# Retention and two feed-forward layers on one core: the first loads on two queues, and TensorE in the program's order during the first tile

## The chip, the cores and the metric

One core of a Trainium2 chip runs the whole program. The metric is the device time of one execution in microseconds (us); each number given as a time of a kernel is a median of several executions, and the trace is that of one further execution. The engines are TensorE (PE in the rows, with PEld for its weight loads), VectorE (DVE), ScalarE (ACT), GpSimd (POOL) and SyncE (SP), which here only issues transfers.

## The reference

Retention over 4 batches, 8 heads, 576 positions and 64 dimensions a head feeds a first feed-forward layer (a gate h*cos(h)) and then a second one (a normalisation, a gate silu(g)*val). Cut to what matters:

```python
scores = scale * np.matmul(q, k.transpose(0, 1, 3, 2))
gamma = 1.0 - 2.0 ** (-5.0 - np.arange(H, dtype=np.float32))
Dmat = np.where(rel >= 0, gamma[:, None, None] ** rel[None, :, :], 0.0)
x = np.matmul(scores * Dmat[None], v)              # -> 2304 tokens x 512
h = x @ w_in                                       # 512 -> 2048
x = (h * np.cos(h)) @ w_out                        # 2048 -> 512
xn = x / np.sqrt(np.mean(x * x, -1, keepdims=True) + 1e-06) * rms_g
g, val = xn @ w_gate, xn @ w_val                   # 512 -> 1536
out = (g * (1.0 / (1.0 + np.exp(-g))) * val) @ w_out2
```

## The kernel before

**Retention.** The 576 positions of a batch are cut into five chunks (four of 128 positions and one of 64), so there are 20 chunks, numbered n. A chunk has one load of 1 MB (`x`: k and q turned, v, and k by tokens), issued on SyncE's queue by `load(n)`. Each chunk is worked in four groups of matrix products, and this text names them by letters:

- S(n), in `scores`: the products of k and q, 8 matmuls into two PSUM banks (L249). VectorE multiplies both banks with the triangular mask (L252, two passes) and so frees them.
- T(n), in `values`: k times v is added to the running sum `total` of the batch (L265). Before it GpSimd has scaled v (L244). ScalarE copies `total` into `state` afterwards (L275), which the next chunk reads; the next T may not add to `total` before that copy.
- Q(n): state times q (L270), except for the first chunk of a batch.
- V(n): masked scores times v (L280). VectorE then multiplies the result with the decay table `gam` into `xall` (L283) and so frees the bank.

The decay tables of the four later chunk positions are made once from the first one (`gam0`, loaded from `gq`) by 16 ScalarE instructions (L237).

**First feed-forward layer.** It goes over tiles of 512 tokens and over 16 blocks f of the hidden width. In the first tile (tokens 0 to 511, thus chunks 0 to 3) a step i does H(i), the product of x with the block's first weights (12 matmuls of 512 columns, L187 to L189), a gate, and O(i-3), the product of the gated block with its second weights (12 matmuls of 512 columns into `acc`). In the program O(f) is written three steps after H(f) (`LAG`). The gate is a chain: ScalarE L414, VectorE L415, ScalarE L417 (a sine), VectorE L421, ScalarE L423, VectorE L124. x and the weights are split into a high and a low part: for x four casts on ScalarE (L181) and four subtractions on VectorE (L124), and for each block a conversion of the loaded words: ScalarE L132 and L141, VectorE L136, L137, L142 and L143, ScalarE L159 and VectorE L124 on `w`. All 16 blocks are converted during the first tile.

**How the two are interleaved.** Chunks 0 to 4 come first, in the loop `for n in range(PRO)`. Chunks 5 to 19 are spread over steps 0 to 7 of the first tile, up to two in a step; the program writes a step as H(i), S, O(i-3), T Q V, S, T Q V.

**What sets the order.** Up to the end of the first tile a scheduler orders each engine's instructions by its own model; the order of the source is not kept, on any engine. From then on ScalarE, VectorE and GpSimd keep to the program's order (`manual_schedule(engines=ENGINES)`), and later TensorE too. During retention the results of S, V and H share three PSUM banks (`g`, `bufs=3`), in the order in which the program takes them. SyncE's queue is in the order of `PLAN`: chunks 0 to 3, block 0, chunks 4 and 5, block 1, and so on. Ahead of everything, 10 matmuls on constants (`WARM`) keep TensorE busy until the first data come.

## Time and profile before

| | |
|---|---|
| median of 3 executions | 930.67 us (929.98 to 932.38) |
| the profiled execution, its own time | 928.54 us |
| its span, from the first to the last instruction | 926.7 us |
| TensorE busy | 903.1 us, 97% of the span |
| VectorE, ScalarE, GpSimd busy | 619.6, 462.2, 26.9 us |

The profiled execution took 1.84 us more than its span, and 2.13 us less than the median. The profile's table of forty slices (each 23 us) shows TensorE below nine tenths in the first and the last alone, and VectorE at eight or nine tenths in the second to the seventh, that is in the first tile.

### The profile page before, as it was taken

To read this page: it belongs to the slowest core of one execution; us is meant where nothing else is said; L and a number is where in the kernel's file an instruction comes from. 1 tells how busy PE (TensorE), PEld (TensorE's weight loads), DVE (VectorE), ACT (ScalarE), POOL (GpSimd) and SP (SyncE) were. 2 spreads that over 40 slices of the span, in tenths; PEclk is the share of its full clock that TensorE was granted. 3 is DMA by queue.
4 is the path that set the end of the run, shared out by engine and by line. 5 is a ranking of instruction groups with operands and counts; after the bars stand their busy time and mean duration, and the time that the engine had idled before them with its cause. 6 is when DMAs were issued, how large, how long until landed. Compare 5 with 4: busy or idle time off the path is not lost.

```text
span 926.7 us, 12891 instructions
## 1 busy us (share of the span) xinstructions
PE 903.1 (97%) x4996; PEld 791.0 (85%) x4996; DVE 619.6 (67%) x1022; ACT 462.2 (50%) x816; POOL 26.9 (3%) x27
## 2 busy tenths in 40 slices
PE   7999999999999999999999899999999999999998
PEld 6777788888887888988888799999888999999997
DVE  3999989778888887768657666675456446333332
ACT  4656566576556666367545444444432334322222
POOL 2321100000000000000000000000000000000000
PEclk9999999999999999999999999999999999999999
DMA  8946451035424353202035376676744555755531
GB/s 334 410 186 227 155 224 72 21 117 193 164 98 159 137 159 126 69 1 103 1 148 204 124 297 251 252 268 246 259 176 176 207 209 212 265 206 209 204 132 69
DMA packets 34732, 163.72 MB, mean 177 GB/s; under 512 B 4080, under 2 KB 5232, under 8 KB 23792
## 3 DMA queue, kind: packets, MB, share of 16 engines
q1 hardware_dynamic: 34672, 162.91, 48.0%
q8 instruction: 39, 0.64, 0.3%
q14 instruction: 21, 0.17, 0.1%
HBM read 123.57 MB, written 39.32 MB: 176 GB/s over the span
## 4 chain that ended last, share of the span: by engine, by line
PE 79%; DVE 14%; ACT 4%; issue 2%; DMA 1%; SPq 0%; ACTq 0%; DVEq 0%
PE h L743 27%; PE acc L715 15%; PE acc L187 8%; PE acc L188 8%; PE acc L189 8%; PE h L189 3%; PE h L188 3%; PE h L187 3%; DVE r L421 1%; DVE t L142 1%; DVE t L143 1%; PE g L280 1%; DVE r L415 1%; PE g L249 1%; PE g L270 1%
## 5 line engine op out<-in xcount | busy, mean ns | idle before, releaser
L743 PE MATMUL h<-w 128*128 128x384 f32 x1224 | 230.5, 337 | 6.6 <-ACT s L750 2.6
L743 PEld LDWEIGHTS h<-w 128*128 128x128 f32 x1224 | 214.9, 188 | 15.2 <-ACT s L750 5.3
L715 PE MATMUL acc<-w,shi 128*128 128x512 f32 x432 | 134.3, 392 | 0.0
L187 PE MATMUL acc<-ghi,w 128*128 128x512 f32 (+1 forms) x320 | 117.4, 373 | 2.8 <-ACT xall L614 1.7
L188 PE MATMUL acc<-glo,w 128*128 128x512 f32 (+1 forms) x320 | 117.6, 369 | 0.1
L189 PE MATMUL acc<-ghi,w 128*128 128x512 f32 (+1 forms) x320 | 117.3, 368 | 0.0
L750 ACT COPY s<-h 128x384 f32<-128x384 f32 x108 | 51.9, 480 | 128.1 <-PE h L743 128.0
L715 PEld LDWEIGHTS acc<-w,shi 128*128 128x128 f32 x432 | 80.1, 188 | 13.4
L417 ACT ACTIVATE r<-r,half_pi 128x512 f32<-128x512 f32 (+1 forms) x80 | 54.5, 681 | 65.5 <-DVE r L415 65.2
L763 DVE TENSOR_TENSOR sg<-s,h 128x384 f32<-128x384 f32 x54 | 29.9, 553 | 85.6 <-PE h L743 45.4
L715 PE MATMUL acc<-w,slo 128*128 128x512 f32 x216 | 85.4, 395 | 0.0
L775 ACT CAST shi<-v 128x384 fp32r<-128x384 f32 x72 | 37.0, 514 | 70.3 <-DVE v L771 70.3
L124 DVE TENSOR_TENSOR glo<-r,ghi 128x512 fp32r<-128x512 f32 (+1 forms) x78 | 49.6, 636 | 33.4 <-ACT ghi L423 31.6
L187 PEld LDWEIGHTS acc<-ghi,w 128*128 128x128 f32 x320 | 59.4, 188 | 14.5 <-ACT xall L614 2.8
L423 ACT CAST ghi<-r 128x512 fp32r<-128x512 f32 (+1 forms) x80 | 46.2, 577 | 48.2 <-DVE r L421 46.9
L189 PEld LDWEIGHTS acc<-ghi,w 128*128 128x128 f32 x320 | 60.3, 188 | 10.1
L188 PEld LDWEIGHTS acc<-glo,w 128*128 128x128 f32 x320 | 60.3, 188 | 10.1 <-DVE glo L124 0.3
L124 DVE TENSOR_TENSOR slo<-v,shi 128x384 fp32r<-128x384 f32 x72 | 40.1, 557 | 37.3 <-ACT shi L775 37.3
L770 DVE TENSOR_TENSOR v<-s,h 128x384 f32<-128x384 f32 x54 | 29.8, 552 | 52.0 <-PE h L743 37.9
L743 PE MATMUL h<-b,w 128*128 128x384 f32 x288 | 56.8, 338 | 0.0
L188 PE MATMUL h<-xlo,w 128*128 128x512 f32 (+1 forms) x148 | 54.3, 367 | 0.1
L189 PE MATMUL h<-xhi,w 128*128 128x512 f32 (+1 forms) x148 | 54.2, 366 | 0.0
(105 smaller groups left out, 1518.6 us busy)
## 6 DMA issues: line engine op xcount, KB each, us to landing
w<-s SPq DMA_DIRECT2D x24, 1024.0 KB, 4.8
raw<-w_dram SPq DMA_DIRECT2D x36, 512.0 KB, 4.0
w<-w SPq DMA_DIRECT2D x18, 1024.0 KB, 5.1
w<-s SPq DMA_DIRECT2D x24, 768.0 KB, 6.4
raw<-w_dram SPq DMA_DIRECT2D x16, 1024.0 KB, 7.1
x<-qkv_dram SPq DMA_DIRECT2D x15, 1024.0 KB, 8.1
s<-w SPq DMA_DIRECT2D x12, 1024.0 KB, 4.8
s<-w SPq DMA_DIRECT2D x12, 768.0 KB, 3.6
```

What stands on the lines that cost most here:

```text
L124: eng.tensor_tensor(dst, src, hi.bitcast(F32), op=ALU.subtract)
L187: nc.tensor.matmul(dst, a[0], b[0], start=start, stop=False)
L188: nc.tensor.matmul(dst, a[0], b[1], start=False, stop=False)
L189: nc.tensor.matmul(dst, a[1], b[0], start=False, stop=stop)
L417: nc.scalar.activation(r, r, AF.Sin, bias=half_pi, scale=1.0)
L423: nc.scalar.copy(hi, r)
L715: nc.tensor.matmul(acc, (hi, hi, lo)[k][:, c], w[:, u, (0, 1, 0)[k], :], start=start and u == 0 and k == 0, stop=stop and u == 1 and k == 2)
L743: nc.tensor.matmul(bank, a[:, wp], xp[:, c], start=start and kc == 0 and n == 0, stop=kc == 1 and n == 2, skip_group_check=True)
L750: nc.scalar.copy(t, alpha)
L763: nc.vector.tensor_tensor(t, s, bank, op=ALU.add)
L770: nc.vector.tensor_tensor(t, s, bank, op=ALU.add)
L775: nc.scalar.copy(hi, t)
```

## The change

The first chunk is loaded in two transfers of 512 KB in place of four of 256 KB; the tables `gk`, `mask` and `gq` go from SyncE's queue to ScalarE's; the second chunk is loaded in two transfers. `WARM` goes from 10 to 8. The decay tables are no longer written in `load` but in a function of their own, called after `values(n)`. And from the first chunk to the end of the first tile TensorE keeps to the program's order, while the other engines are ordered by the scheduler as before.

```diff
--- before.py
+++ after.py
@@ -60,7 +60,7 @@
 NSLOT_B = NW1 - NSLOT_A
 ATT_STEPS = 8
 CONV_LEAD = 3
-WARM = 10
+WARM = 8
 AHEAD = 4
 LAG = 3
 LAST_BEGINS = [48, 51, 54, 65, 66, 67]
@@ -221,9 +221,13 @@
         b, c = chunks[n]
         x = wa.tile([P, 4, DM], F32, tag="w", name="x")
         if n == 0:
-            for src, dst in ((qkv[b, c, :, 0], x[:, 0]), (qkv[b, c, :, 1], x[:, 1]), (gk, gk_sb), (mask, mask_sb),
-                             (qkv[b, c, :, 2], x[:, 2]), (gq, gam0), (qkv[b, c, :, 3], x[:, 3])):
-                nc.sync.dma_start(dst, src)
+            for eng, src, dst in ((nc.sync, qkv[b, c, :, :2], x[:, :2]), (nc.scalar, gk, gk_sb),
+                                  (nc.scalar, mask, mask_sb), (nc.sync, qkv[b, c, :, 2:], x[:, 2:]),
+                                  (nc.scalar, gq, gam0)):
+                eng.dma_start(dst, src)
+        elif n == 1:
+            nc.sync.dma_start(x[:, :2], qkv[b, c, :, :2])
+            nc.sync.dma_start(x[:, 2:], qkv[b, c, :, 2:])
         elif c < NFULL:
             nc.sync.dma_start(x, qkv[b, c])
         else:
@@ -231,10 +235,12 @@
             nc.sync.dma_start(x[:REST, 2], vr[b])
         blocks = lambda a: a[:, :NPAIR * width(c)].rearrange("p (a i) -> p a i", a=NPAIR)
         ld[n] = blocks(x[:, 0]), blocks(x[:, 1]), x[:, 2], x[:, 3]
-        if 0 < n < NCH:
-            gam.append(ap1.tile([P, NPAIR, width(c)], F32, name=f"gam{c}"))
-            for p in range(NPAIR):
-                nc.scalar.activation(gam[c][:, p, :], gam0[:, p, :width(c)], AF.Copy, scale=later[:, c, p:p + 1])
+
+    def decay(c):
+
+        gam.append(ap1.tile([P, NPAIR, width(c)], F32, name=f"gam{c}"))
+        for p in range(NPAIR):
+            nc.scalar.activation(gam[c][:, p, :], gam0[:, p, :width(c)], AF.Copy, scale=later[:, c, p:p + 1])

     def scores(n):
         b, c = chunks[n]
@@ -299,12 +305,17 @@
             else:
                 load(n)

+
+    order = ExitStack()
+    order.enter_context(tc.manual_schedule(engines={mybir.EngineType.PE}))
     fetch(1)
     scores(0)
     for n in range(PRO):
         fetch(n + AHEAD)
         scores(n + 1)
         values(n)
+        if n + 1 < NCH:
+            decay(n + 1)
         if n == 3:
             split_x(ORDER_A[0])
             blocks1[0].convert(temps())
@@ -679,7 +690,7 @@
             late["cv"] = right("cv", 3)
             piece_load(0)
             piece_load(1)
-            order = ExitStack()
+            order.close()
             order.enter_context(tc.manual_schedule(engines=ENGINES))
         if i == LAST_BEGINS[-1] + 1:
             assert len(begins) == npiece and not valued
```

On ScalarE's queue, at the start of the program (`gam_91` is `gam0`), before:

```order
L237 ACT_TABLE_LOAD
L237 ACTIVATE gam_121<-gam_91,gk_sb 128x128 x4
L237 ACTIVATE gam_143<-gam_91,gk_sb 128x128 x4
L237 ACTIVATE gam_150<-gam_91,gk_sb 128x128 x4
L237 ACTIVATE gam_160<-gam_91,gk_sb 128x64 x4
L275 COPY state<-total 64x4x64 x4
```

and now:

```order
L227 DMA gk_sb<-gk_dram 128x60
L227 DMA mask_sb<-mask_dram 128x128
L227 DMA gam_91<-gq_dram 128x512
L243 ACT_TABLE_LOAD
L243 ACTIVATE gam_176<-gam_91,gk_sb 128x128 x4
L243 ACTIVATE gam_218<-gam_91,gk_sb 128x128 x4
L243 ACTIVATE gam_262<-gam_91,gk_sb 128x128 x4
L243 ACTIVATE gam_304<-gam_91,gk_sb 128x64 x4
L281 COPY state<-total 64x4x64 x4
```

Three transfers stand ahead; the 16 table instructions still stand in one piece ahead of the first copies of `state`, although the source now writes them after the chunks.

On TensorE, from the end of H(0) (the first row of each piece) to the start of H(1), which ends the piece before with L187 and L188 on `g`, before:

```order
L189 MATMUL g<-xhi,w 128x512
L249 MATMUL g<-x 128x128 x4
L280 MATMUL g<-s_351,x 64x128
...
L265 MATMUL total<-x 128x128 x4
L249 MATMUL g<-x 128x128 x8
L270 MATMUL g<-x,state 128x128 x4
L280 MATMUL g<-s_449,x 64x128
...
L265 MATMUL total<-x 128x128 x4
L187 MATMUL acc<-ghi,w 128x512
...
L187 MATMUL g<-xhi,w 128x512
L188 MATMUL g<-xlo,w 128x512
L249 MATMUL g<-x 128x128 x8
```

and now:

```order
L189 MATMUL g<-xhi,w 128x512
L255 MATMUL g<-x 128x128 x8
L271 MATMUL total<-x 128x128 x4
L286 MATMUL g<-s_350,x 64x128
...
L255 MATMUL g<-x 128x128 x8
L271 MATMUL total<-x 128x128 x4
L276 MATMUL g<-x,state 128x128 x4
L286 MATMUL g<-s_448,x 64x128
...
L187 MATMUL g<-xhi,w 128x512
L188 MATMUL g<-xlo,w 128x512
```

The 12 products of O(0) (on `acc`) stood between T(7) and H(1), and S(8) inside H(1); now nothing stands between V(6) and H(1), and O(0) has gone to its written place behind H(3).

On VectorE, from the mask passes of chunk 6 in the gate of H(0) to the subtraction on `w` that H(1) needs, before:

```order
L283 TENSOR_TENSOR xall<-g,gam_91 128x4x128
L421 TENSOR_TENSOR r<-g,r 128x512
L143 ISA t<-raw,t 128x2048
L252 TENSOR_TENSOR s_484<-g,mask_sb 128x512
L124 TENSOR_TENSOR glo<-r,ghi 128x512
L252 TENSOR_TENSOR s_486<-g,mask_sb 128x512
L283 TENSOR_TENSOR xall<-g,gam_121 128x4x128
L136 TENSOR_SCALAR t<-t 128x1024
L137 TENSOR_SCALAR t<-t 128x1024
L142 SCALAR_TENSOR_TENSOR t<-raw,t 128x1024
L143 ISA t<-raw,t 128x2048
L124 TENSOR_TENSOR w<-t,w 128x2x512
```

and now:

```order
L258 TENSOR_TENSOR s_450<-g,mask_sb 128x512
L432 TENSOR_TENSOR r<-g,r 128x512
L289 TENSOR_TENSOR xall<-g,gam_91 128x4x128
L143 ISA t<-raw,t 128x2048
L124 TENSOR_TENSOR glo<-r,ghi 128x512
L258 TENSOR_TENSOR s_483<-g,mask_sb 128x512
L258 TENSOR_TENSOR s_485<-g,mask_sb 128x512
L136 TENSOR_SCALAR t<-t 128x1024
L137 TENSOR_SCALAR t<-t 128x1024
L289 TENSOR_TENSOR xall<-g,gam_176 128x4x128
L142 SCALAR_TENSOR_TENSOR t<-raw,t 128x1024
L124 TENSOR_TENSOR w<-t,w 128x2x512
```

The passes are the same in number and nearly in order; the subtraction on `w` of block 1 moved ahead of L143 of block 2. From step 9 of the first tile to the end of the program TensorE's instructions stand in the same order in both kernels.

## Rows read from the trace of the kernel before

**Rows 1.** The page: each engine's busy time, its share and its count.
```profile
PE 903.1 (97%) x4996; PEld 791.0 (85%) x4996; DVE 619.6 (67%) x1022; ACT 462.2 (50%) x816; POOL 26.9 (3%) x27
```

**Rows 2.** Busy time by stretch: length, then each engine's busy us and count, PEclk, DMA.
```profile
38.60:72.80 34.20, 32.44 (x298) 27.25 (x296) 32.76 (x42) 22.93 (x30) 7.12 (x6) 1.00 0.61 234
72.80:130.80 58.00, 56.04 (x488) 46.24 (x487) 54.57 (x72) 33.05 (x47) 6.03 (x5) 1.00 0.49 179
```

**Rows 3.** The timeline of the opening: start, length, instruction, count, idle before.
```profile
2.10 4.59 PE L290 MATMUL idle_bank<-warm,ones_r 128*128 128x512 f32 x10 [2.10 <-DVE warm L287]
...
3.07 0.43 SPq L226 DMA_DIRECT2D gam<-gq_dram  x1
...
4.02 1.54 SPq L228 DMA_DIRECT2D x<-qkv_dram  x3
...
8.10 1.28 ACT L237 ACT_TABLE_LOAD   x1 [8.10 <-DMA gam<-gq_dram]
...
9.39 4.57 ACT L237 ACTIVATE gam<-gam,gk_sb 128x128 f32<-128x128 f32 x16
...
13.95 1.04 POOL L244 TENSOR_TENSOR x<-x,gk_sb 128x512 f32<-128x512 f32 x1 [1.40 <-DMA x<-qkv_dram]
...
14.75 0.68 PE L265 MATMUL total<-x 128*128 128x128 f32 x4 [1.09 <-ACT state L275]
```

**Rows 4.** Two stretches of the opening; the last two columns are DMA share and GB/s.
```profile
1.50:6.50 5.00, 4.40 (x10) 3.14 (x10) 0.46 (x1) 0.00 (x0) 0.00 (x0) 1.00 0.77 220
7.50:11.50 4.00, 1.43 (x16) 1.08 (x12) 1.29 (x2) 3.39 (x9) 0.98 (x1) 1.00 1.03 420
```

**Rows 5.** The timeline from the end of chunk 3 to the first gate.
```profile
27.19 0.69 DVE L283 TENSOR_TENSOR xall<-g,gam 128x512 f32<-128x512 f32 x1 [0.50 <-PE g L280]
...
27.91 1.14 ACT L181 CAST xhi<-xall 128x512 fp32r<-128x512 f32 x2 [0.95 <-DVE xall L283]
...
28.96 1.17 ACT L132 ACTIVATE t<-raw 128x1024 f32<-128x1024 f32 x1
...
30.54 1.04 ACT L159 CAST w<-t 128x1024 fp32r<-128x1024 f32 x1
...
31.63 0.50 PE L187 MATMUL g<-xhi,w 128*128 128x512 f32 x1 [0.66 <-ACT w L159]
...
38.61 0.69 DVE L415 SCALAR_TENSOR_TENSOR r<-r,g 128x512 f32<-128x512 int32 x1
```

**Rows 6.** One stretch inside H(0), columns as in rows 2.
```profile
34.00:37.00 3.00, 3.00 (x8) 2.33 (x8) 2.96 (x5) 0.07 (x1) 1.05 (x1) 0.50 1.00 405
```

**Rows 7.** TensorE's timeline: a V, the first and last record around O(0).
```profile
43.48 1.09 PE L280 MATMUL g<-s,x 128*64 128x128 f32 x16
...
45.43 0.48 PE L187 MATMUL acc<-ghi,w 128*128 128x512 f32 x1
...
48.27 0.39 PE L187 MATMUL g<-xhi,w 128*128 128x512 f32 x1
```

**Rows 8.** VectorE's timeline: block 2 converted, and the gate of H(1).
```profile
45.23 0.69 DVE L136 TENSOR_SCALAR t<-t 128x1024 f32<-128x1024 f32 x1
45.95 0.69 DVE L137 TENSOR_SCALAR t<-t 128x1024 int32<-128x1024 int32 x1
46.68 1.23 DVE L142 SCALAR_TENSOR_TENSOR t<-raw,t 128x1024 int32<-128x1024 int32 x1
47.94 1.23 DVE L143 CUSTOM_DVE_ANT_0 t<-raw,t 128x2048 uint16<-128x2048 uint16 x1
49.09 1.22 DVE L124 TENSOR_TENSOR w<-t,w 128x1024 fp32r<-128x1024 f32 x1
...
55.40 0.68 DVE L415 SCALAR_TENSOR_TENSOR r<-r,g 128x512 f32<-128x512 int32 x1
```

**Rows 9.** TensorE's timeline: its longest wait after H(0), and the start of H(8).
```profile
57.86 0.67 PE L249 MATMUL g<-x 64*64 64x64 f32 x8 [1.34 <-DVE r L421]
...
130.84 0.40 PE L187 MATMUL h<-xhi,w 128*128 128x512 f32 x1
```

## The prediction

> **What bounds the kernel now.** I read the page first, then the busy time by stretch, then the timeline of the first 60 us, and last the order of the instructions in both kernels. TensorE is busy for 97% of the span [rows 1], and every matmul but two of the warm-up is kept, so the time can only change by what TensorE waits and by the clock it is granted. The reader is to see two stages in the first tile. From H(0)'s end to H(3), 38.6 to 72.8, VectorE is busy 32.76 of 34.20 us, and TensorE still waits for only 34.20-32.44 = 1.76 us [rows 2], because it is handed O(0) and O(1) early: O(0) stands at 45.43 to 48.27 [rows 7], before H(1). From 72.8 to H(8) at 130.84 [rows 9] it waits 58.00-56.04 = 1.96 us [rows 2]. From step 9 on both kernels have one order on TensorE, so I walk the new order up to H(8) and carry the shift found there to the end.
>
> **Durations.** S, T, Q and V take 1.0 to 1.1 us each (V runs 43.48 to 44.55) and the 64-wide ones 0.6; O takes 48.27-45.43 = 2.84, so 0.237 a record, and H, also 12 records, about 2.95 with the change to the next product [rows 7]. VectorE's small passes start 0.6 to 0.7 apart, L142 1.25, L143 1.15, the subtraction on w 1.15 [rows 8].
>
> **The opening.** Now T(1) starts at 14.75, released by the copies of `state` [rows 3]. Those stand on ScalarE behind the table load (8.10, released by `gq`) and 16 table instructions (9.39, 4.57 us): 5.85 us from `gq`'s landing to the copies, 0.75 for them. In the new order S(2) stands before T(1), so T(1) needs the later of two things.
> First the load of chunk 2, which lands at 13.95 now (GpSimd's start, [rows 3]). Its issue comes some 2.4 us earlier, since 4.02 was chunk 1's issue behind seven smaller ones and two transfers now precede it. But the DMA engines were already busy 0.77 of the time from 1.5 to 6.5, at 220 GB/s; later they are full at 420 [rows 4]. Filling the free share gives 5 x 0.23 = 1.1 us; moving the same 1.1 MB at 420 GB/s gives 5-2.6 = 2.4. I take the middle, 1.75: landing 12.2, S(2) done at 13.3.
> Second `gq`: now issued at 3.07 and landed at 8.10. Third on ScalarE's queue it is issued at about 1.65 (0.43 per issue); with the 5.0 us that it took (3.07 to 8.10) it lands at 6.6; if it gains chunk 2's 1.75 as well, at 4.9; with no gain, at 8.0. Two of the three lie low, but it shares the engines with chunk 0, so I take 6.2: copies done at 6.2+5.85+0.75 = 12.8. So S(2) decides and T(1) starts at 13.3; with `gq` at 8.0 it would be 14.6.
> The Trainium skill, "DMA: Bandwidth & Descriptors", section "Rules for kernel authors", speaks against this part: it says that spreading transfers over several issuing engines gives no bandwidth, since all run on the same 16 DMA engines, and saves issue time alone. The share of 0.77 [rows 4] agrees in kind; by the rule only the free 1.1 us is to be had, and the sum below would be 0.65 higher.
> The two warm-up matmuls (4.59/10 = 0.46 each, [rows 3]) save nothing: TensorE then waits longer for chunk 1.
>
> **From T(1) to the first gate.** From 14.75 to V(3)'s end (27.14, where the decay pass at 27.19 is released, [rows 5]) lie 12.4 us, 1.1 of them S(2), which is done already: 13.3+11.3 = 24.6, a gain of 2.55. The decay pass (0.65) ends at 25.3. ScalarE's row is now cast, L132, cast, L159, cast, L141, cast: 4 x 0.57 + 1.07 + 0.95 + 1.07 = 5.4 [rows 5], to 30.7. VectorE's last subtraction on x, then L136, L137, L142: 0.6+2.6, to 34.0. There L415 of the first gate starts, against 38.61 [rows 5]: 4.6 earlier. H(0) waits for L159 and for w and ends at 32.2.
>
> **What TensorE then waits for.** This is the price of the program's order.
> To H(1): its third product needs block 1's subtraction on w. From 34.0 VectorE has eleven small passes (6.85), L143, L142 and the subtraction (3.55): 44.4. TensorE has, from 32.2, only S(6) T(5) V(5) S(7) T(6) Q(6) V(6) and two products of H(1): 8.0 us. It waits 4.2. H(1) ends at 46.8.
> To H(2): Q(7) shares its bank with S(8) and needs the mask pass of chunk 8, which stands behind L143, L136, L137, the subtraction, L142, the gate's L415 and another L143: 7.25, so 51.65. TensorE has S(8) and T(7), to 49.0, and waits 2.6. Then Q(7) V(7), a wait of 0.25 for L421, S(9) T(8) Q(8) V(8): H(2) starts at 57.85.
> To H(3): Q(9) waits 0.8 for a mask pass behind the gate of H(2), S(11) waits 0.65 for that gate's L421. H(3) starts at 68.25.
> Together 8.5 us of waits against 1.76. Behind the waiting product everything on TensorE queues up, and O(0), whose data have long been there, is among it.
>
> **The sum.** H(3) starts 72.8-68.25 = 4.55 earlier. But TensorE owes 23 of the 24 records of O(0) and O(1), 5.45 us, and three quarters of T(11), 0.8 us, that stood ahead of H(3) before. From H(3) on each step holds an O: TensorE has 2.95+2.84+2x4.2 = 14.2 us of work in it, VectorE 10.5 (two chunks at 1.85, a gate at 1.8, a conversion at 4.95), and walking the order I find no wait, so the 1.96 fall away. The least slack is Q(14), 0.3 us. Shift at H(8): -4.55+5.45+0.8-1.96 = -0.3.
> Two things are still missing. VectorE's passes from 38.61 to 55.40 [rows 5, 8] sum to 15.7 by the spacings above and took 16.8: 1.1 of slower passes and hops, which I expect again in the stretch where VectorE bounds. And in H(0) TensorE ran at the lower of its clock levels (granted 0.50, eight records in 3.00 us, [rows 6]) after a wait of 0.66 us and a shorter one; now it waits about 1.1 (V(4) ends at 27.4, L159 at 28.5) and 0.7 there. At 0.43 a record (the ten warm-up products, 4.59 with the last one's tail, [rows 3]) in place of 0.237 the ten records behind w cost 1.95, of which 1.0 is covered by VectorE, busy until 34.0: 0.95 on the path.
> Sum: -0.3+1.1+0.95 = +1.75. The profiled execution of 928.54 becomes 930.3; the median of the runs shown lies 2.13 above that execution, so I predict **932.4** from 930.67. The measurement tells a change from none at about 0.3%, 2.8 us: this is no change.
> Bounds: chunk 2's landing ±0.65, `gq` up to +1.3, VectorE's extra 0 to 1.1, the clock 0 to 0.95. That is from -0.95 to +3.7: the forecast's own range is 929.7 to 934.4.
>
> **The rivals.**
> *VectorE stays the bound beyond H(3).* With the slack of 0.3 at Q(14), a VectorE 1 us later brings waits back in steps 4 to 6. Before, that stage had 1.96 us of waits though TensorE could choose its order; if they return and half as much again, +2 to +3 on the sum, some 935. For it: VectorE is busy 54.57 of 58.00 there [rows 2]. Against: each step then has an O of 2.84 us to cover it. It decides once VectorE is 0.3 us late at chunk 13.
> *Slower, by a warm-up that is too short.* Eight matmuls end at about 5.7. If the clock has not risen by then, S(1), T(0), V(0) and S(2) run at the lower level, 0.8 us more each, 3.2, less 0.6 of waiting for chunk 2: +2.6, some 935. For it: all ten of now ran at the lower level to their end (0.46 each, [rows 3]), so nothing shows that eight are enough. Against: TensorE goes on to S(0) at once. It decides when T(1) starts after 13.3.
> *Faster, because the early O were worth nothing.* If VectorE, 4.6 earlier, gets block 1's subtraction done by 40.2 in place of 44.4, the waits fall to about the 1.76 of before: 8.5-1.76 = 6.7 less, some 925.7. Against: the passes in front of it are the same in number as in the rows, and only half of the gap could come from any reordering.
> *The queues do nothing.* `gq` at 8.0 and chunk 2 later by 0.65: T(1) at 14.6, +1.3, some 933.7.
>
> **Chances.** The forecast 0.50; VectorE the bound for longer 0.16; the short warm-up 0.14; the early O worth nothing 0.14; the queues without effect 0.06. The forecast's range and the last case lie partly above 933.5: of their 0.56 about 0.07 are slower, and 0.01 faster. So faster 0.15, same 0.48, slower 0.37. The range that leaves out 2 in 10 takes in the two slower cases up to 936 and a part of the faster one: 927.3 to 936.3.
>
> **What would show it.** Chunk 2's scaling on GpSimd near 12.2, ScalarE's table load near 6.2, T(1) near 13.3; the first gate's L415 near 34 to 35; a wait of TensorE ahead of H(1)'s third product, and one of 2 to 3 us ahead of Q(7), each ended by VectorE; O(0) behind H(3) at 74 to 76; H(8) at 132.5. I am wrong if T(1) comes after 14, if the waits between H(0) and H(3) sum to less than 6 or more than 11 us, if waits of more than 1 us stand between H(3) and H(8), or if the clock is granted at 0.50 anywhere but in H(0).

## The result, and the profile after

The changed kernel takes 937.37 us (936.03 to 940.93, 6 runs) beside 930.62 for the kernel before in the same runs: ratio 1.0078, interval 1.0059 to 1.0097. It is 6.75 us slower; 932.4 was forecast, and the range ended at 936.3.

The recorded profile is of the longest of the six runs (940.93, mean granted clock 0.987; the others 0.990 to 0.991). So the changed kernel was profiled once more in the experiments, at 937.45; where sizes matter both are given, the first one first.

The opening, in the timeline of the changed kernel (the columns are those of [rows 3]):

```profile
1.66 0.45 ACTq L227 DMA_DIRECT2D gam<-gq_dram  x1
...
9.15 1.28 ACT L243 ACT_TABLE_LOAD   x1 [9.15 <-DMA gam<-gq_dram]
...
12.39 1.04 POOL L250 TENSOR_TENSOR x<-x,gk_sb 128x512 f32<-128x512 f32 x1 [1.47 <-DMA x<-qkv_dram]
...
14.92 0.74 ACT L281 COPY state<-total 64x256 f32<-64x256 f32 x2
...
15.76 1.41 PE L271 MATMUL total<-x 128*128 128x128 f32 x8 [2.13 <-issue]
16.96 1.92 PE L276 MATMUL g<-x,state 128*128 128x128 f32 x8
```

Chunk 2 lands at 12.4 as forecast (12.2). `gq` was issued 1.4 us earlier than in [rows 3] and lands 1.05 us later. ScalarE's chain behind it is as long as before, so T(1) starts at 15.76 instead of 13.3, after a wait of 2.13 us; its row names no releaser ("issue"), but the copies of `state` end at 15.66, just ahead of it. Q(1), which takes about 1.06 elsewhere, takes 1.92.

TensorE's timeline from H(1) to H(3), cut to the waits and to the records at half rate:

```profile
47.99 0.50 PE L187 MATMUL g<-xhi,w 128*128 128x512 f32 x1 [0.95 <-ACT w L159]
...
50.87 0.80 PE L189 MATMUL g<-xhi,w 128*128 128x512 f32 x1 [2.14 <-DVE w L124]
51.46 0.63 PE L187 MATMUL g<-xhi,w 128*128 128x512 f32 x1
...
55.90 1.16 PE L271 MATMUL total<-x 128*128 128x128 f32 x8
59.51 1.16 PE L276 MATMUL g<-x,state 128*128 128x128 f32 x8 [2.45 <-DVE s L258]
...
72.55 1.08 PE L276 MATMUL g<-x,state 128*128 128x64 f32 x8 [1.66 <-DVE s L258]
...
76.79 2.07 PE L271 MATMUL total<-x 128*128 128x128 f32 x8
78.79 1.98 PE L286 MATMUL g<-s,x 128*64 128x128 f32 x16
80.70 0.77 PE L187 MATMUL g<-xhi,w 128*128 128x512 f32 x1
```

The reader sees the forecast waits in the forecast places: ahead of H(1)'s third product, of Q(7) and of Q(9), all ended by VectorE (2.14, 2.45 and 1.66 us; 4.2, 2.6 and 0.8 were forecast). A wait of 0.95 ahead of H(1)'s first product, ended by ScalarE, was not forecast. Behind them the records stand 0.43 apart in place of 0.23, and T(10) and V(10) take 2.0 in place of 1.1. The same in windows (columns as in [rows 2]; the first three rows are stages, the others lie inside stretches granted half the clock):

```profile
0.00:15.76 15.76, 9.48 (x81) 7.47 (x81) 5.54 (x11) 6.47 (x19) 4.46 (x9) 1.00 0.88 346
15.76:80.70 64.94, 55.09 (x469) 45.78 (x469) 53.34 (x68) 34.15 (x48) 13.21 (x12) 0.82 0.71 264
80.70:142.26 61.56, 60.12 (x514) 50.55 (x513) 53.44 (x69) 33.10 (x47) 7.16 (x5) 0.99 0.46 161
...
16.50:19.00 2.50, 2.50 (x14) 2.28 (x14) 0.00 (x0) 0.03 (x1) 0.00 (x0) 0.50 1.09 315
33.50:40.00 6.50, 5.79 (x20) 4.07 (x20) 5.63 (x8) 2.33 (x4) 1.30 (x2) 0.50 1.01 367
50.90:53.90 3.00, 3.00 (x7) 2.42 (x8) 2.96 (x3) 1.05 (x1) 1.56 (x1) 0.50 0.66 276
61.00:64.00 3.00, 3.00 (x33) 2.55 (x30) 2.42 (x6) 2.61 (x5) 0.00 (x0) 0.50 0.85 309
74.50:81.00 6.50, 6.44 (x41) 5.43 (x40) 4.37 (x8) 2.62 (x5) 0.00 (x0) 0.50 0.45 161
```

The lower level, which [rows 6] show once before H(8), stands at five places. H(8) starts at 142.26 beside 130.84 [rows 9]. The same stages in the second profile:

```profile
0.00:15.54 15.54, 10.14 (x80) 8.09 (x81) 5.55 (x11) 6.48 (x19) 4.18 (x9) 1.00 0.88 344
15.54:76.84 61.30, 51.06 (x468) 42.50 (x468) 54.24 (x68) 33.28 (x48) 13.14 (x12) 0.89 0.74 281
76.84:138.54 61.70, 59.88 (x514) 50.32 (x513) 54.37 (x69) 34.80 (x48) 7.30 (x5) 1.00 0.45 160
```

TensorE waits 64.94-55.09 = 9.85 and 61.30-51.06 = 10.24 us between T(1) and H(3). The two runs hold the same work there, but one is busy 4.03 longer, with (1-0.82) x 2 x 64.94 = 23.4 us at half the clock against 13.5: 0.41 us lost for each us at the lower level. The stage from H(3) to H(8) is about as long as forecast, 61.6 and 61.7 for 62.3.

### The profile page after: what moved, and what is told of

Its sections match the earlier page's. It is cut to its first block, busy times and chain, and to the rows that moved or that the text cites. A ratio compares the mean times of both kernels' runs of the same rounds, so it can differ in the third digit from the quotient of the medians.

```text
span 938.8 us, 12888 instructions
## 1 busy us (share of the span) xinstructions
PE 908.0 (97%) x4994; PEld 795.6 (85%) x4994; DVE 620.2 (66%) x1022; ACT 462.2 (49%) x816; POOL 27.8 (3%) x27
## 4 chain that ended last, share of the span: by engine, by line
PE 79%; DVE 14%; ACT 3%; issue 2%; DMA 1%; SPq 0%; ACTq 0%; DVEq 0%
PE h L754 26%; PE acc L726 15%; PE acc L187 8%; PE acc L188 8%; PE acc L189 8%; PE h L187 3%; PE h L188 3%; PE h L189 3%; DVE t L142 2%; PE g L286 2%; DVE t L143 1%; DVE r L432 1%; PE g L255 1%; PE total L271 1%; PE g L276 1%
## 5 line engine op out<-in xcount | busy, mean ns | idle before, releaser
L187 PE MATMUL acc<-ghi,w 128*128 128x512 f32 (+1 forms) x320 | 117.3, 373 | 2.8 <-ACT xall L625 1.7
L188 PE MATMUL acc<-glo,w 128*128 128x512 f32 (+1 forms) x320 | 117.5, 369 | 0.1
L726 PEld LDWEIGHTS acc<-w,shi 128*128 128x128 f32 x432 | 80.1, 188 | 13.5
L124 DVE TENSOR_TENSOR glo<-r,ghi 128x512 fp32r<-128x512 f32 (+1 forms) x78 | 51.3, 658 | 34.6 <-ACT ghi L434 32.8
L187 PEld LDWEIGHTS acc<-ghi,w 128*128 128x128 f32 x320 | 59.3, 188 | 14.8 <-ACT xall L625 2.7
L189 PEld LDWEIGHTS acc<-ghi,w 128*128 128x128 f32 x320 | 60.3, 188 | 10.2
L188 PEld LDWEIGHTS acc<-glo,w 128*128 128x128 f32 x320 | 60.3, 188 | 10.1 <-DVE glo L124 0.3
L124 DVE TENSOR_TENSOR slo<-v,shi 128x384 fp32r<-128x384 f32 x72 | 40.1, 557 | 37.3 <-ACT shi L786 37.3
L188 PE MATMUL h<-xlo,w 128*128 128x512 f32 (+1 forms) x148 | 54.3, 367 | 0.1
L187 PE MATMUL h<-xhi,w 128*128 128x512 f32 (+1 forms) x148 | 54.3, 367 | 0.0
```

Of the source, the lines that this page charges most:

```text
L124: eng.tensor_tensor(dst, src, hi.bitcast(F32), op=ALU.subtract)
L187: nc.tensor.matmul(dst, a[0], b[0], start=start, stop=False)
L188: nc.tensor.matmul(dst, a[0], b[1], start=False, stop=False)
L189: nc.tensor.matmul(dst, a[1], b[0], start=False, stop=stop)
L726: nc.tensor.matmul(acc, (hi, hi, lo)[k][:, c], w[:, u, (0, 1, 0)[k], :], start=start and u == 0 and k == 0, stop=stop and u == 1 and k == 2)
```

## The experiments

Starts in us from each profile; "low" is the time at half the clock up to H(8), worked out from windows of half a microsecond; the warm-up is not in it, since the granted column shows 1.00 there [rows 4] although its products took 0.46 us each. The ratios are against the kernel before, measured along with each run.

| kernel | median | ratio, interval | T(1) | H(3) | H(8) | low |
|---|---|---|---|---|---|---|
| before | 930.62 | | 14.75 | 72.79 | 130.84 | 3.4 |
| changed | 937.37 | 1.0078, 1.0059-1.0097 | 15.76 | 80.70 | 142.26 | 23.9 |
| e16 changed again | 938.01 | 1.0080, 1.0060-1.0100 | 15.54 | 76.84 | 138.54 | 13.7 |
| e1 loads alone | 936.88 | 1.0058, 1.0045-1.0070 | 15.67 | 79.09 | 139.28 | 13.7 |
| e2 order alone | 941.71 | 1.0107, 1.0094-1.0121 | 17.17 | 80.48 | 142.10 | 17.1 |
| e3 gq first | 939.33 | 1.0084, 1.0070-1.0097 | 15.73 | 78.57 | 140.14 | 20.5 |
| e4 early O | 937.49 | 1.0065, 1.0052-1.0077 | 15.87 | 83.17 | 139.98 | 20.5 |
| e5 fill | 939.47 | 1.0112, 1.0091-1.0134 | 15.91 | 78.20 | 142.72 | 13.7 |
| e6 ten warm-up products | 939.34 | 1.0104, 1.0083-1.0125 | 15.62 | 79.91 | 141.54 | 17.1 |
| e7 queues, old order | 928.26 | 0.9980, 0.9966-0.9994 | 12.83 | 71.22 | 128.51 | 0 |
| e8 gq alone on ScalarE | 929.77 | 0.9995, 0.9983-1.0008 | 16.29 | 76.12 | 133.14 | 10.2 |
| e9 scores inside H | 942.66 | 1.0120, 1.0099-1.0141 | 16.21 | 80.10 | 144.29 | 27.3 |
| e10 inside, early O | 938.01 | 1.0074, 1.0060-1.0089 | 15.88 | 82.03 | 139.18 | 13.7 |
| e11 the same, queues | 938.30 | 1.0081, 1.0061-1.0100 | 17.08 | 80.81 | 141.94 | 23.9 |
| e12 e7, chunk 1 split | 934.73 | 1.0037, 1.0022-1.0051 | 14.22 | 78.06 | 138.33 | 10.2 |
| e13 lead two | 936.93 | 1.0070, 1.0045-1.0095 | 15.73 | 75.08 | 136.09 | 17.1 |
| e14 lead two, early O | 935.43 | 1.0037, 1.0021-1.0052 | 15.67 | 78.58 | 137.24 | 10.2 |
| e15 e7, lead two | 926.76 | 0.9955, 0.9938-0.9972 | 12.99 | 69.56 | 128.76 | 0 |
| e17 O one step behind | 932.64 | 1.0016, 1.0001-1.0031 | 15.87 | 72.80 | 136.89 | 10.2 |
| e18 e17, queues, ten | 931.34 | 1.0005, 0.9993-1.0017 | 16.26 | 73.43 | 136.34 | 6.8 |

A start says nothing by itself: e4, e10, e11, e14, e17 and e18 have O(0) and O(1) done at H(3), 5.7 us of TensorE's work, like the kernel before; the other kernels in the written order have none of it. At H(8) e17 and e18 have seven O done, the others five.

In e3, e6 and e16 TensorE's and VectorE's instructions up to H(8) stand in the changed kernel's order, but for e6's two warm-up products. In e2, e4, e5, e9 to e11, e13, e14, e17 and e18 the scheduler wrote VectorE's in another order, so each of these tests its edit together with that order.

### Which half loses

**e1**, the changed kernel without the line that fixes TensorE's order in the first tile:

```diff
-    order.enter_context(tc.manual_schedule(engines={mybir.EngineType.PE}))
```

> The changed kernel without the written order on TensorE in the first tile: new loads, tables and eight warm-up products alone. My theory (the loss is the late landing of gq, plus the waits of the written order, plus the lower clock behind those waits): gq lands near 9.2 again, T(1) starts near 15.7, 1.0 later than before, and TensorE, free to choose, waits no more than before behind it; one or two stretches at the lower clock; 931 to 933. Rival one (the loads or the short warm-up carry the whole loss): 936 to 938. Rival two (the loads gain and the order alone loses): under 930.

**e2**, the kernel before with that line and nothing else:

```diff
+    order = ExitStack()
+    order.enter_context(tc.manual_schedule(engines={mybir.EngineType.PE}))
     fetch(1)
```

> The kernel before with the written order on TensorE in the first tile and nothing else of the change. My theory: T(1) at 14 to 15 and V(3) at 27 to 28; TensorE waits 6 to 8 us between H(0) and H(3), ahead of H(1), Q(7) and Q(9), ended by VectorE, and runs at the lower clock in three to six stretches; H(8) at 138 to 141; 935 to 937. If the loads or the short warm-up were the loss: 930 to 932, whatever waits show.

The order alone costs 10.0 us (931.68 to 941.71), more than the whole change and more than I expected. The loads alone cost 5.2, in the range of rival one and against my theory: T(1) came where I had it, but TensorE waited 3.76 us for a mask pass ahead of Q(7). Two losses of 10.0 and 5.2 do not make one of 6.75, so something else changed with the loads. Part of it is the opening: in e2 T(1) starts at 17.17, 2.4 later than before, because the written order has S(1) ahead of T(0) and TensorE waits 4.19 us there for chunk 1; with the change's loads T(1) starts at 15.5 to 15.8. And in e1 the scheduler, free again on TensorE, had written another order than before; e7 and e12 take this apart.

**e7** is the kernel before, with chunk 0 in two transfers, `gk` and `mask` on ScalarE's queue, and `gq` on SyncE's between the halves of chunk 0. TensorE's order up to H(8) is that of before; chunk 1 is one piece. **e12** adds to it what the change does to chunk 1:

```diff
-            for src, dst in ((qkv[b, c, :, 0], x[:, 0]), (qkv[b, c, :, 1], x[:, 1]), (gk, gk_sb), (mask, mask_sb),
-                             (qkv[b, c, :, 2], x[:, 2]), (gq, gam0), (qkv[b, c, :, 3], x[:, 3])):
+            for eng, src, dst in ((nc.sync, qkv[b, c, :, :2], x[:, :2]), (nc.scalar, gk, gk_sb),
+                                  (nc.scalar, mask, mask_sb), (nc.sync, gq, gam0),
+                                  (nc.sync, qkv[b, c, :, 2:], x[:, 2:])):
...
+        elif n == 1:
+            nc.sync.dma_start(x[:, :2], qkv[b, c, :, :2])
+            nc.sync.dma_start(x[:, 2:], qkv[b, c, :, 2:])
```

(The last three lines are e12's alone.)

> The kernel before, TensorE's and VectorE's order as it was, with chunk 0 in two transfers, gk and mask on ScalarE's queue, and gq on SyncE's queue between the two halves of chunk 0 (chunk 1 in one piece, ten warm-up products). Theory one (the loads gain in themselves and lose through the order that follows from them): gq lands at 4.5 to 6, T(1) starts at 12.3 to 13.5, the order of before keeps TensorE fed, and the time is 1 to 2.5 us under the kernel before, 928.5 to 930.5 beside its 931. Rival one (VectorE's stage or the clock swallows it): no difference within 1 us. Rival two (the loads cost in themselves, as in the run of the loads alone): 933 or more.

> The kernel that was faster than the one before (queues changed, order of before kept) with one thing more: chunk 1 in two transfers. That alone makes the scheduler write another order on TensorE and VectorE in the first tile, the one it had in the run of the loads alone. My theory (the loads alone lost 5 us through that order and not through the transfers): T(1) at 12 to 14, a wait of 3 us or more ahead of Q(7), and 932 to 935, 4 to 6 over the kernel without the split. Rival (the loss was gq's late landing in the opening): 927.5 to 929.5.

e7 gains 2.2 us, and in its profiled execution, one of the fastest of twelve, the lower level is not granted up to H(8). Its timeline:

```profile
6.17 1.28 ACT L236 ACT_TABLE_LOAD   x1 [6.17 <-DMA gam<-gq_dram]
...
12.83 0.68 PE L264 MATMUL total<-x 128*128 128x128 f32 x4 [0.61 <-ACT state L274]
```

`gq`, issued at 1.19 and landed by 6.17, no longer holds T(1) up for long. e12 loses 6.5 against e7 by the medians (5.3 by the ratios), with T(1) only 1.4 later, and waits where e1 waited (its TensorE):

```profile
52.41 0.40 PE L189 MATMUL acc<-ghi,w 128*128 128x512 f32 x1
55.92 1.16 PE L272 MATMUL g<-x,state 128*128 128x128 f32 x8 [3.11 <-DVE s L254]
```

TensorE's instructions up to H(8) stand in e12 in e1's order, but for two warm-up products. So e1 lost through the order that the split of chunk 1 made the scheduler write, and loads of this kind are worth 2.2 us in the old order. Under the written order the change's own loads are worth about the same (1.0107-1.0078, 2.7 us). The order is where the time goes.

### The opening

**e3** puts `gq` first on ScalarE's queue, **e8** is the kernel before with `gq` alone there and `gk` and `mask` on SyncE's, **e6** is the changed kernel with ten warm-up products. (Of each transfer of e3 and e8 only the queue and the target are shown, in order.)

```diff
e3 -(nc.sync, x[:, :2]), (nc.scalar, gk), (nc.scalar, mask), (nc.sync, x[:, 2:]), (nc.scalar, gq)
e3 +(nc.scalar, gq), (nc.sync, x[:, :2]), (nc.scalar, gk), (nc.scalar, mask), (nc.sync, x[:, 2:])
e8 +(nc.scalar, gq), (nc.sync, x[:, :2]), (nc.sync, gk), (nc.sync, mask), (nc.sync, x[:, 2:])
e6 -WARM = 8
e6 +WARM = 10
```

> The changed kernel with gq issued first on ScalarE's queue, ahead of gk and mask (issue near 0.7 in place of 1.66). My theory (a transfer's landing goes by what is queued ahead of it when it is issued): gq lands at 5 to 7, T(1) starts near 13.3 as the prediction had it, the lower clock around T(1) to V(1) is gone, the first gate comes 2 to 3.5 us earlier, and the time is 933 to 935. Rival (the shared engines serve it late whatever its place): it lands near 9, T(1) near 15.7, 937.

> The kernel before, TensorE's order as it was, with gq alone on ScalarE's queue, issued near 0.7, and chunk 0 in two transfers on SyncE's queue with gk and mask between them. Theory one: gq lands at 4 to 6, T(1) at 12.3 to 13.5, 1 to 2.5 us under the kernel before. If ScalarE's queue is what makes gq late: it lands at 8 or later, T(1) at 14.5 or later, and the time is that of before within 1 us.

> The changed kernel with ten warm-up products again in place of eight. If the short warm-up is a cause: no stretch granted 0.50 ahead of V(1), T(1) about 1 to 2 earlier where there was one, and 933 to 936. My theory (chunk 1 and gq set the opening, the lower clock follows the waits for them): the waits ahead of S(1) shrink by what the two products take, T(1) stays at 15.5 to 16, a stretch at 0.50 remains between 8 and 20, and the time is that of the changed kernel within 1 us, 936.5 to 939.

From issue to landing `gq` took 7.4 us third on ScalarE's queue, 5.3 first on it (e3), 4.3 alone on it (e8), 4.9 on SyncE's behind one half of chunk 0 (e7): the place decides. But e3 gained nothing, against my theory. T(1) no longer waits, yet starts at 15.73, because T(0) and V(0) run at half rate behind two waits for chunk 1 and its mask pass:

```profile
8.67 0.48 PE L255 MATMUL g<-x 64*128 64x128 f32 x2 [0.91 <-DMA x<-qkv_dram]
9.88 1.22 PE L255 MATMUL g<-x 64*128 64x128 f32 x14 [0.73 <-DVE s L258]
11.03 2.08 PE L271 MATMUL total<-x 128*128 128x128 f32 x8
13.03 1.67 PE L286 MATMUL g<-s,x 128*64 128x128 f32 x16
14.63 1.16 PE L255 MATMUL g<-x 64*128 64x128 f32 x16
15.73 1.16 PE L271 MATMUL total<-x 128*128 128x128 f32 x8
```

e8 missed its T(1) in the same way: `gq` is in time, but chunk 0 comes late, T(0) waits 2.85 us (for GpSimd's scaling of chunk 0), and all from T(0) to V(0) takes double; the time is that of before. e6 refutes the short warm-up as the cause: T(1) stays, and the kernel is no faster.

### What in the order loses

**e4** writes O(0) ahead of H(1) and O(1) ahead of H(3). **e5** fills TensorE's waits with products of constants into the idle bank, and so adds work that yields nothing. **e9** writes S(6), S(8), S(10) inside the hidden products, **e10** does that and e4's edit, **e11** adds e7's queues. (Of e5 and e9 the main lines are shown.)

```diff
e4 +            if i in (1, 3):
e4 +                out_t(*steps[i // 2])
e4              ps = hidden(t, f)
...
e4 -        if i >= LAG:
e4 +        if i >= LAG + 2:
e5 +FILL = {'S1': 4, 'S2': 3, 'T1': 7, 'H0': 4, 'H0w': 2, 'H1': 3, 'H1w': 8, 'Q7': 9, 'Q9': 6}
...
e5 +        for _ in range(FILL.get(place, 0)):
e5 +            nc.tensor.matmul(idle_bank, ones_r, src, start=True, stop=True)
e9 +            if amid and kc == 0:
...
e9 +                nc.tensor.matmul(dst[:, :n], whi[:, c], xlo[:, :n], start=False, stop=False)
e9 +                amid()
e9 +                nc.tensor.matmul(dst[:, :n], wlo[:, c], xhi[:, :n], start=False, stop=False)
...
e9 +            amid = (lambda: scores(more[0] + 1)) if i < 3 else None
```

> The changed kernel with O(0) written ahead of H(1) and O(1) ahead of H(3), where the scheduler had them before, in place of behind H(3) and H(4). My theory (the late O leave TensorE nothing to do in VectorE's stage): the waits ahead of H(1) fall from 3.1 to under 1 us, those ahead of Q(7) and Q(9) stay or shrink by a part, one or two stretches at the lower clock fewer; H(3) starts at 81 to 83 with both O done, H(8) 3 to 5 us earlier; 932 to 934.5. Rival (the waits are VectorE's alone and only move): 936.5 to 938.

> The changed kernel with extra products of constants into the idle bank just where TensorE waits in it: 4 and 3 ahead of S(1) and S(2), 7 ahead of T(1), 4 and 2 inside H(0), 3 and 8 inside H(1), 9 ahead of Q(7), 6 ahead of Q(9); 46 of about 0.24 us, 11 us of work that yields nothing. Theory one (behind each wait the clock falls, and the work done at half rate is a loss besides the wait): H(1), Q(7) and Q(9) are released by VectorE no later than in the changed kernel, the stretches granted 0.50 ahead of H(3) fall from five or more to two at most, and the time is 933 to 935. Rival (the waits alone cost; the clock is made up for by them): 937 to 940, the fillers running over what they fill.

> The changed kernel with S(6), S(8) and S(10) written inside H(0), H(1) and H(2), between the second and the third product, in place of behind them. My theory (the written order starts these scores only behind the product that waits for VectorE, so that their mask passes and with them Q(7) and Q(9) come late): the wait ahead of H(1)'s third product falls from 2.1-2.9 to 1-2, those ahead of Q(7) and Q(9) from 2.5 and 1.7 to under 0.5, H(2) starts at 62 to 64 in place of 66 to 67, one or two stretches at the lower clock fewer; 933 to 935 beside 931 for the kernel before. Rival (VectorE has the same passes to do, so the waits only move): 936.5 to 939.

> The last kernel's S(6), S(8) and S(10) inside the hidden products, and besides O(0) written ahead of H(1) and O(1) ahead of H(3), as in the run of the early O. My theory (the two together are what the scheduler's order had over the written one): no wait over 1.5 us between H(0) and H(3), H(3) starts at 78 to 80 with both O done, and 930.5 to 933. If the early O is worth no more than the 1.3 that it gave alone, and the scores nothing: 936 to 937.5.

> The last kernel with the queues of the run that was faster than the kernel before: gq on SyncE's queue between the two halves of chunk 0, chunk 1 in one piece. If the loads and the order add up: 2 to 3 us under the last kernel, T(1) at 12.5 to 14. If a late chunk or the lower clock takes that back: the time of the last kernel within 1 us.

e4 took the wait ahead of H(1)'s third product from 2.14 to 1.01 and that of 0.95 before it away, but the one ahead of Q(7) grew from 2.45 to 3.99. It gained 1.2 to 1.4 us by the ratios (against the changed kernel and e16), as the rival had it. e5 kept the clock at full rate up to Q(9), and H(2) started at 62.4 (66.8 and 63.1 in the changed kernel's two profiles). Then VectorE was 2.19 us late for Q(9) and, here, 1.78 for Q(14), and the clock fell at both:

```profile
104.41 1.72 PE L292 MATMUL g<-x,state 128*128 128x64 f32 x8 [1.78 <-DVE xall L305]
...
107.71 0.63 PE L194 MATMUL g<-xlo,w 128*128 128x512 f32 x1
```

Its time lies in the rival's range. So the time at the lower clock is not simply given back to a TensorE that is kept busy: here it waits for VectorE afterwards. Two things blur this run. VectorE's passes stand in another order, and the eight products ahead of H(1)'s third one run 1.7 us past the subtraction that it needs (47.71 to 49.40); but Q(7) stands on VectorE's mask pass again behind that. e9 is 4 us slower than the changed kernel, against my theory: Q(7) and Q(9) no longer wait, but S(9) and S(11), behind Q(7) and Q(9), wait 3.14 and 2.05 us for VectorE. e10 is e9 mended by the early O, no better than e4, and e11's loads gave nothing there, T(1) coming at 17.08 behind products at half rate.

What e4 left is on VectorE, in the changed kernel's timeline:

```profile
55.06 2.06 DVE L142 SCALAR_TENSOR_TENSOR t<-raw,t 128x1024 int32<-128x1024 int32 x1
57.04 0.67 DVE L426 SCALAR_TENSOR_TENSOR r<-r,g 128x512 f32<-128x512 int32 x1
57.64 1.21 DVE L143 CUSTOM_DVE_ANT_0 t<-raw,t 128x2048 uint16<-128x2048 uint16 x1
58.77 1.28 DVE L258 TENSOR_TENSOR s<-g,mask_sb 128x512 f32<-128x512 f32 x2
```

S(8) ends at 55.9, but its mask pass stands behind a gate pass and two conversion passes of later blocks. In these rows VectorE does not wait; the pass stands where the scheduler's order has it.

**e13** therefore sets CONV_LEAD, the steps by which conversions run ahead, to 2 in the changed kernel. **e14** is that with e4's edit, **e15** is e7 with CONV_LEAD at 2, **e16** the changed kernel as it is.

```diff
-CONV_LEAD = 3
+CONV_LEAD = 2
```

> The changed kernel with CONV_LEAD at 2 in place of 3: a block of weights is converted for the hidden product two steps on, and TensorE's order is the same. On VectorE the passes of block 3 leave the place ahead of chunk 8's mask pass. My theory (the order on VectorE sets when Q(7) and Q(9) run): the wait ahead of Q(7) falls from 2.5 to under 1, H(2) starts at 62 to 64.5 in place of 66 to 67, H(3) at 76 to 78, and the time is 931.5 to 935. Rival (VectorE has the same passes to do and the waits trade places, at a later H or at Q(14) and Q(16)): 936.5 to 939.

> The last kernel with O(0) written ahead of H(1) and O(1) ahead of H(3) as well. Theory (with VectorE in order, work for TensorE in its waits counts): no wait over 1.5 us between H(0) and H(3), H(3) at 79 to 81 with both O done, 929.5 to 932.5. Rival (as in the runs with the early O so far, VectorE's sum is the bound): 935.5 to 938.

> The kernel that was faster than the one before (its queues, the scheduler free on TensorE) with CONV_LEAD at 2; the scheduler's order up to H(2) is the one of before, behind it other. If conversions written too early cost something there as well: 925.5 to 927.5, under the kernel with 3. If the scheduler had already put the urgent passes first: 927.5 to 929.5, no difference. If a block comes late: over 930, with a wait of an H for w.

> The changed kernel once more, as it is. Its time should be 936 to 939 again; a profile from the middle of its times should have five stretches at the lower clock in place of seven, T(1) near 15.7, the waits ahead of H(1), Q(7) and Q(9) of 2 to 3 us each as in the first, and H(3) at 79 to 80.

e16 confirms the changed kernel's time; its profile has H(3) earlier than I expected, with less of the lower clock. In e13 Q(7) waits no more, H(2) starts at 61.2 and H(3) at 75.1, 0.8 and 0.9 ahead of what I expected. Q(9) waits, as it does in e16 (e13's TensorE; its row names ScalarE's sine, but VectorE's mask passes of chunk 10 run at that time, from 66.33 to 67.61):

```profile
55.51 1.16 PE L276 MATMUL g<-x,state 128*128 128x128 f32 x8
...
64.18 1.16 PE L255 MATMUL g<-x 64*128 64x128 f32 x16
67.15 1.08 PE L276 MATMUL g<-x,state 128*128 128x64 f32 x4 [1.81 <-ACT r L428]
```

The time is hardly lower (936.93, from 933.63 to 942.32, 0.9 by the ratios against e16): it lies in the rival's range. With the early O besides, e14 gains 4 us over the changed kernel by the ratios, less than I expected, and keeps waits of 2.33 ahead of Q(9) and 1.89 behind H(3). e15 is the best kernel of all, 926.76.

**e17** puts an O at just these places: CONV_LEAD at 2, O(0) ahead of H(1), and each O one step behind its gate, so that O(1) stands between S(10) and Q(9). **e18** adds e7's queues and ten warm-up products.

```diff
+            if i == 1:
+                out_t(*steps[0])
             ps = hidden(t, f)
...
-        if i >= LAG:
+        if 2 <= i <= 8:
+            out_t(*steps[i - 1])
+        elif i >= 11:
             out_t(*steps[i - LAG])
```

> The changed kernel with CONV_LEAD at 2, O(0) written ahead of H(1), and from step 2 to step 8 O of the step before in place of that of three steps before, so that O(1) stands between S(10) and Q(9) and O(2) between S(12) and T(11). My theory (what the written order lacks is O at the places where VectorE is behind): the waits ahead of Q(9) and Q(11), 2.3 and 1.9 in the last run with early O, fall under 0.5, H(8) starts with O(0) to O(6) done at 139 to 142, and the time is 930 to 933. Rival (VectorE's sum bounds the first tile, and O at any place only moves the wait): 934.5 to 937.

> The last kernel with gq on SyncE's queue between the two halves of chunk 0, chunk 1 in one piece, and ten warm-up products. If the loads and the order add up: 2 to 3 us under the last kernel, 928 to 931, with no stretch at the lower clock ahead of H(0). If the opening only waits for VectorE later: the time of the last kernel within 1 us.

e17's TensorE, with the first and the last record of O(1):

```profile
64.10 1.16 PE L255 MATMUL g<-x 64*128 64x128 f32 x16
65.19 0.50 PE L187 MATMUL acc<-ghi,w 128*128 128x512 f32 x1
...
67.83 0.39 PE L189 MATMUL acc<-ghi,w 128*128 128x512 f32 x1
68.05 1.00 PE L276 MATMUL g<-x,state 128*128 128x64 f32 x8
...
72.80 0.50 PE L187 MATMUL g<-xhi,w 128*128 128x512 f32 x1
```

The wait ahead of Q(9) is gone, filled by work that has to be done anyway, and the low stretch behind it with it (another came at 101, so "low" is 10.2 beside e16's 13.7). H(3) starts at 72.80 with both O done: 72.79 was the kernel before. The time is 932.64: of the 7.4 us that a ratio of 1.0080 means (e16), 6.0 are back (1.0016); against e13, which has CONV_LEAD at 2 and no O moved, 5.0 (1.0070). e18 adds 1.0 and is level with the kernel before; I had expected 2 to 3, but its S(1) waits 2.44 us for chunk 1 and T(0) and V(0) run at half rate.

## Why the prediction was wrong

It forecast +1.75 in place of about +7. By its own steps, with e16's profile, which lies near the median:

- **Chunk 2 and the two products of the warm-up**: right. 12.2 was forecast for chunk 2's landing and 12.4 measured, and the share of the DMA engines from 1.5 to 6.5 rose from 0.77 to 0.87. By the rule of the Trainium skill, "DMA: Bandwidth & Descriptors", section "Rules for kernel authors", it would have been 12.85; the row lies nearer to the forecast.
- **"`gq` ... so I take 6.2"**: failed, and "with no gain, at 8.0" was no bound either. It landed at 9.15 and 8.9. I took its transfer time of before and let the earlier issue carry over; in fact it took 7.4 in place of 5.0. T(1) came 2.2 us late.
- **"1.1 of slower passes and hops" on VectorE**: the term that failed most. From the first gate to Q(9) VectorE set the pace, as forecast, but with the passes just ahead of that gate its walk took 4.0 us longer than by the spacings (the table and the rows below).
- **"0.95 on the path" for the clock**: wrong in place and in size. I gave the lower level to H(0) alone, from [rows 6], though I had just put waits of 4.2 and 2.6 us, longer than the one ahead of [rows 6], at two more places. In e16 the half rate of H(0) and H(1) costs nothing on the path, since VectorE, which shows no wait from 29.22 to 62.78, is later still. From Q(9) to H(3) TensorE has no wait, and there it costs 3.0 by the forecast's durations.

| from the step before (or the start) to | forecast, us | e16, us | what is longer |
|---|---|---|---|
| T(1) | 13.3 | 15.54 | `gq` |
| the first gate's second pass (L415, now L426) | 20.7 | 21.58 | L142 at 35.25 |
| H(1)'s third product | 10.4 | 11.19 | L124 at 41.34 |
| Q(7) | 7.25 | 8.77 | L136 at 49.31, L124 at 51.49 |
| Q(9) (62.7 by its durations) | 11.05 | 11.88 | L136 at 64.94 |
| H(3) | 5.55 | 7.88 | half rate, 3.0; a forecast wait of 0.65 did not come |
| H(8) | 62.3 | 61.70 | |

VectorE's long passes in e16's timeline, and the first of TensorE's records at half rate behind them:

```profile
35.25 1.95 DVE L142 SCALAR_TENSOR_TENSOR t<-raw,t 128x1024 int32<-128x1024 int32 x1
37.12 0.68 DVE L426 SCALAR_TENSOR_TENSOR r<-r,g 128x512 f32<-128x512 int32 x1
...
41.34 1.53 DVE L124 TENSOR_TENSOR glo<-r,ghi 128x512 fp32r<-128x512 f32 x1
...
49.31 1.53 DVE L136 TENSOR_SCALAR t<-t 128x1024 f32<-128x1024 f32 x1
...
51.49 2.07 DVE L124 TENSOR_TENSOR w<-t,w 128x1024 fp32r<-128x1024 f32 x1
...
64.94 1.53 DVE L136 TENSOR_SCALAR t<-t 128x1024 f32<-128x1024 f32 x1
...
68.96 1.84 PE L276 MATMUL g<-x,state 128*128 128x64 f32 x8 [1.76 <-DVE s L258]
```

Each of the five is 0.7 to 0.85 us longer than its kind usually is, 4.1 in all, and each lies beside GpSimd's scaling of a chunk. The 1.1 was read off a stretch of the kernel before in which two passes were 0.25 longer; L137 at 35.81, 0.73 longer, stands just ahead of that stretch. The gate at 37.12 follows L142 without a wait, while H(0) at half rate and ScalarE behind it had ended at 36.87. (In the first profile half rate lasts through H(0), and there the gate waits 0.80 us for it.)

- **What TensorE then waits for**: right in place and, for the most part, in releaser; that the sum of 8.5 came out near (7.2 and 7.9 measured) was in part luck. VectorE was later than forecast and TensorE, at half rate, slower, so that the gap between them stayed.
- **The sum from H(3) to H(8)**: 61.7 for 62.3, but by luck. "I find no wait" was wrong: waits of 0.65 and 1.17 us stood there, ahead of Q(14) and Q(16), while TensorE's work took 59.88 in place of 62.3. Three records of O(5), 0.7 us, which the kernel before has done ahead of H(8), were not taken off in the forecast.

T(1) +2.2, VectorE 4.0 in place of 1.1, Q(9) to H(3) +2.3 in place of 0.95 and the last stage -0.6 make +5.9 over the forecast at H(8) (138.54 for 132.6); the medians differ by 5.6.

These are the terms of the miss, not the cause of the loss: VectorE has long passes beside GpSimd in the kernel before as well. That TensorE's written order loses is shown by e2 and e7; what e17 took back is time in VectorE's stage in which TensorE had no work of its own. The clock has a part that no run isolates: e5 kept it up and was not faster, but of the twelve executions of the changed kernel the two with a mean granted clock of 0.987 took 940.9 and 941.0 us and the ten with 0.989 to 0.993 from 936.0 to 938.7.

Of the rivals, the short warm-up fell (e6). "The queues do nothing" was right for T(1) and more than that: 2.2 us of the miss. T(1) stayed at 15.5 or later in all runs with the written order, e3 too, so what an earlier one would be worth there is open; beside the kernel before it is only 0.8 to 1.0 late. VectorE as the bound beyond H(3) showed in e5, not in the changed kernel's sum. "The early O were worth nothing" is refuted: with the later conversions e17's O are worth 5.0 us (e13 to e17). Of my four signs of being wrong three came true (T(1), a wait of 1.05 and 1.17 us ahead of Q(16), the clock outside H(0)); the waits from H(0) to H(3) stayed within 6 to 11.

What stays open: what e17's places for O are worth with CONV_LEAD at 3, and how much of its gain is the O and how much VectorE's other order (early O alone, e4, and later conversions alone, e13, gave 1.4 and 0.9 against e16 by ratio, within the intervals; e14 with both 4.0); and why e6 with two products more is 2 us slower than the changed kernel by medians, where the intervals overlap.

## What to carry to other kernels

Where one engine waits for another through a whole stage, independent work that is written late can cost up to its own length: the waits stay empty, and it is done afterwards (here 5.0 us, e13 to e17; two O are 5.7 us of work). Write it at the very instruction that waits (e4, at other places, gained 1.2 to 1.4), and look which passes the waited-for engine has put ahead of the one that matters. Price that engine's passes by what runs beside them, not by their usual spacing. An order fixed on one engine, or a load split in two, lets a scheduler write the other engines anew, so compare all orders before pricing an edit (e12: one split, 5 to 6.5 us). Time a small transfer by what shares the engines with it when it is issued, not by its issue: the same 256 KB took 4.3 to 7.4 us by its place.

## What the runs showed of the hardware

- The same kernel is granted the lower level at different places from run to run: in the first profile of the changed kernel around T(1), H(0), H(1), S(9) and S(11), in the second around H(0), H(1) and S(11) alone, with waits at the same places, alike to within 0.7 us. The time up to H(8) differs by 3.7 us (142.26 and 138.54).
- Waits of 1.25, 1.32 and 1.09 us in the opening of the kernel before were followed by full rate, and waits of 0.91 and 0.73 us in e3's opening by half rate. The length of the last wait alone does not tell which.
- VectorE's L142 took 2.06 us in place of 1.23 [rows 8] at 55.06 in the first profile, while GpSimd scaled a chunk (54.92 to 56.04), and L136 1.53 in place of 0.69 in e16 at 49.31 beside the scaling at 49.09. Up to H(8) all eleven of e16's passes that took 0.2 to 0.9 us longer than usual overlap a scaling; thirty others that overlap one do not take longer.
